# A Fourier transform feeding an MLP on one core: three folds and eight first-stage copies of batch 0 move to VectorE

## The chip, the core and the metric

The kernel runs on one core of a Trainium2 chip. The metric is the device time of one execution in microseconds; lower is better. The engines are TensorE (PE in the rows, with its weight loads as PEld), VectorE (DVE), ScalarE (ACT), GpSimd (POOL) and SyncE (SP), which here issues most DMAs. A trailing q (SPq, ACTq) is an engine's queue of DMA issues.

## The reference

Eight batches of 3008 x 256 go through a two-dimensional Fourier transform, of which the real part is kept, and then through a two-layer MLP with a piecewise activation:

```python
X = np.fft.fft(x, axis=1); X = np.fft.fft(X, axis=2)
x = X.real.reshape(8 * 3008, 256)
h = x @ w_in                                   # 256 x 2048
g = np.where(h >= 1, h, np.where(h <= -1, 0.0, (h + 1) ** 2 / 4))
out = g @ w_out                                # 2048 x 256
```

The weights come as 64-bit floats.

## The kernel before

The transform along the sequence is split into 47 x 64. Per batch there are eight inputs `x` of 96 x 2 x 512. **Stage one** (`stage1`, L258) multiplies each by a constant matrix on TensorE (L270) and writes the sums `s` into one PSUM bank per piece; four copies (L280) take each bank apart into the tile `z`, two for each half h of the partitions and each part m. `nyquist` (L285) computes `ny` from one column of `z`, copies it (`nyt`, L290) and sends it through DRAM (`nyr`, `nyb`). **Stage two** (`stage2`, L299) multiplies slices of the complete `z` (L309, PSUM tiles also named `s`) and splits each result into a high part `pqh` (ScalarE) and a low part `pql` (VectorE), both in `split` (L168). The transform along the columns is folded into `w_in`.

An input has two planes that are added. `fold_x` (L126) does the adding on GpSimd (L131, tile `y`) for all inputs of later batches and for the odd ones of batch 0; for the even ones of batch 0 TensorE gets both planes and accumulates twice as many matmuls. One float32 matmul leaves two records in the trace.

**Weights.** The 64-bit weights arrive as 16 blocks `raw`; `convert_w` (L192) makes float32 of a block by bit operations, mostly on VectorE (L210 to L225), with a conversion (L208) and, for some, a Relu (L215) on ScalarE. `fold_w_in` (L240) multiplies a pair of blocks by the column transform (`wps`, L246) and splits it into `wh` and `wl`; `fold_delta` (L249) makes `delta` from `dps` (L255); `split_w_out` makes `woh` and `wol`. Blocks 0 and 1 are converted first, then 4, 5, 2 and 3, and the others one by one between the units of the MLP.

**MLP.** A unit is one batch, one third of its columns and 128 of the 2048 features. `gemm1` (L350) makes `uv` on TensorE (L359), then `us` and two halves of `h` on VectorE (L362, L364, L365), `a` on ScalarE (L372, L373), `h` again on VectorE (L374), `gh` on ScalarE (L375) and `gl` on GpSimd (L378). `gemm2` (L382), four units later, adds to `acc` (L402). Batch 0 goes through the features in two visits, so that it can start before all weights are there.

**What sets the order.** `LOADS`, `START` and `NEXT` write out the beginning by hand (x an input's load, p a piece of the transform, c a conversion, f and d the folds of w_in and delta). A scheduler then places each engine's instructions by their dependencies and its own estimates, and puts in the waits; TensorE's order is kept as written within `START`. Each engine works strictly in its order, so an instruction that waits holds up what stands behind it. Tiles with one tag share a number of buffers, and a new tile waits until an old one is read.

Of the kernel before, what the change touches and what calls it, by code (L numbers as in the profile page):

```python
# [12 lines left out]
AF = mybir.ActivationFunctionType  # L13
ALU = mybir.AluOpType
# [84 lines left out]
CV = {0: ("gh", 4), 1: ("gh", 4), 4: ("gh", 4), 5: ("gh", 4), 2: ("a", 3), 3: ("h", 3)}  # L99


VECTOR_RELUS = (0, 1, 4, 5)

EARLY_BANKS = 24
# [5 lines left out]
def fft_ffn_kernel(ctx: ExitStack, tc: tile.TileContext, x, cst, w_in, w_out, out):  # L110
    nc = tc.nc
# [14 lines left out]
    def fold_x(b, q):  # L126

        t = xt.pop((b, q))
        if b or q % 2:
            y = sb.tile([96, CH], F32, tag="y", name=f"y_{b}_{q}", bufs=3)  # L130
            nc.gpsimd.tensor_tensor(y, t[:, 0], t[:, 1], op=ALU.add)  # L131
            yt[b, q] = [y]
        else:
            yt[b, q] = [t[:, 0], t[:, 1]]
        if q == 0:
            y = sb.tile([96, NA], F32, tag="yd", name=f"yd_{b}", bufs=1)
            nc.gpsimd.tensor_tensor(y, t[:, 0, :NA], t[:, 1, :NA], op=ALU.subtract)
            yt[b, "d"] = y
# [22 lines left out]
    def fft_bank(b, name):  # L161

        if b == 0 and early[0] < EARLY_BANKS:
            early[0] += 1
            return ps.tile([P, CH], F32, tag=f"acc{early[0] % 4}", name=name, bufs=1)
        return ps.tile([P, CH], F32, tag="fft", name=name, bufs=1)
# [25 lines left out]
    def convert_w(n):  # L192
# [15 lines left out]
        nc.scalar.activation(lowf, low, AF.Copy, scale=2.0**-52)  # L208
        if n in VECTOR_RELUS:
            nc.vector.tensor_scalar(exp, high, 20, 0x7FF, op0=ALU.logical_shift_right, op1=ALU.bitwise_and)  # L210
# [47 lines left out]
    def stage1(b, q):  # L258
        for p in range(q, min(q + 2, XC)):
            if (b, p) in xt and (b, p) not in yt:  # L260
                fold_x(b, p)
        if q == 0:
            zt[b] = sb.tile([P, NC, P + 1], F32, tag="z", name=f"z_{b}", bufs=1)
        z, y = zt[b], yt[b, q]
        bank = fft_bank(b, f"s1_{b}_{q}")
        pt = bank[:, : GPC * 96].rearrange("p (i n) -> p i n", i=GPC)
        for i in range(GPC):
            for j, part in enumerate(y):
                lhs = part[:, i * P : (i + 1) * P]
                mm = nc.tensor.matmul(pt[:, i], lhs, bm[:96, :], start=(j == 0), stop=(j == len(y) - 1))  # L270
                if i == 0:
                    pinned(b, mm)
        if q == 0:
            pd = bank[:NA, GPC * 96 : GPC * 96 + 2 * NC]
            nc.tensor.matmul(pd, yt[b, "d"], bm[:96, : 2 * NC], start=True, stop=True)  # L275
        for h in range(2):
            for m in range(2):
                src = pt[h * NA : (h + 1) * NA].rearrange("p i (t m c) -> p m c (i t)", t=2, m=2)[:, m]
                dst = z[m * NA : (m + 1) * NA, :, (2 * q + h) * 8 : (2 * q + h + 1) * 8]
                nc.scalar.activation(dst, src, AF.Copy)  # L280
        if q == 0:
            for m in range(2):
                nc.scalar.activation(z[m * NA : (m + 1) * NA, :, P], pd[:, m * NC : (m + 1) * NC], AF.Copy)
# [32 lines left out]
    def pinned(b, matmul):  # L316

        if b:
            tc.keep_in_program_order(matmul)

    def fft_pieces(b):
        pieces = []
        for q in range(XC):
            pieces.append((4, lambda q=q: stage1(b, q)))
        pieces.append((2, lambda: nyquist(b)))
        for h in range(NC // 4):
            pieces.append((4, lambda h=h: stage2(b, h)))
        return pieces
# [6 lines left out]
    for b in range(NB):  # L335
        visits = 1 if b else 2
        m = NFT // visits
# [86 lines left out]
    for _ in range(7):  # L424
# [4 lines left out]
    steps = {  # L429
        "x": lambda n: load_x(0, n),  # L430
        "y": lambda n: fold_x(0, n),
        "p": lambda n: first[n][1](),
        "l": load_w,
# [18 lines left out]
    for i in range(n_units + LAG):  # L452
        run_steps(STEPS.get(i, ""))
        if i < n_units:
            b, r = divmod(i, per)
# [75 lines left out]
```

## Time and profile before

| what | value |
|---|---|
| time, median of three runs | 1764.74 us (1764.58 to 1770.89) |
| the profiled execution, its time | 1765.38 us |
| its span in the trace | 1763.6 us |
| TensorE busy | 1735.8 us (98%) |
| VectorE busy | 1440.0 us (82%) |
| ScalarE busy | 1346.3 us (76%) |
| GpSimd busy | 1202.1 us (68%) |

Busy matmul time is modelled, so a full TensorE is not one at its peak. The start, up to about 200 us, in which weights are converted beside the MLP, looks different from the rest; the shares are averages over both.

### The profile page before, as it was taken

What the parts mean: (1) busy time and instruction counts of PE and PEld (TensorE: products, weight loads), DVE (VectorE), ACT (ScalarE), POOL (GpSimd) and SP (SyncE); (2) the same over time, 40 slices, a digit from 0 to 9 for tenths busy, and PEclk for the clock granted to TensorE, in tenths of its full rate; (3) what the DMA queues carried; (4) which work ended last, traced back from release to release, by engine and by line L of the source; (5) the groups of instructions that cost most, each with busy time, mean ns of one, the idle gap of its engine ahead of it and who ended that gap; (6) DMA issues with size and microseconds to landing.
All of it is one profiled execution on the core that took longest, in us unless ns stands there. A gap on an engine that the chain in (4) does not pass through costs nothing.

```text
span 1763.6 us, 21942 instructions
## 1 busy us (share of the span) xinstructions
PE 1735.8 (98%) x7982; PEld 1420.5 (81%) x7982; DVE 1440.0 (82%) x1766; ACT 1346.3 (76%) x1580; POOL 1202.1 (68%) x838
## 2 busy tenths in 40 slices
PE   9988999999999999999999999999999999999998
PEld 6766888888888788888888888888888888888877
DVE  6999788888887888878888788878888788888887
ACT  5777877777777877777778877788778787777776
POOL 1545966776768766787667876677676766667775
PEclk9999999999999999999999999999999999999999
DMA  7013321010010100110001100011000000000000
GB/s 230 12 66 101 101 104 60 28 50 30 13 51 28 53 30 1 51 48 33 30 10 51 50 28 24 22 39 50 28 24 34 1 23 32 11 25 5 19 25 24
DMA packets 29963, 72.51 MB, mean 41 GB/s; under 512 B 2976, under 2 KB 8224, under 8 KB 29856
## 3 DMA queue, kind: packets, MB, share of 16 engines
q1 hardware_dynamic: 29568, 70.08, 12.1%
q8 instruction: 62, 1.02, 0.2%
q10 hardware_dynamic: 288, 1.05, 0.2%
q14 instruction: 45, 0.37, 0.1%
HBM read 43.31 MB, written 27.81 MB: 40 GB/s over the span
## 4 chain that ended last, share of the span: by engine, by line
PE 61%; ACT 10%; POOL 9%; issue 6%; DVE 5%; ACTq 0%; POOLq 0%; DVEq 0%
PE acc L402 38%; PE uv L359 19%; POOL gl L378 9%; DVE h L374 4%; ACT a L373 4%; ACT gh L375 3%; ACT a L372 3%; PE s L270 2%; PE s L309 2%; ACT z L280 1%; DVE o L414 0%; DVE h L365 0%; DVE h L364 0%; POOL y L131 0%; ACT o L412 0%
## 5 line engine op out<-in xcount | busy, mean ns | idle before, releaser
L378 POOL TENSOR_TENSOR gl<-h,gh 128x512 fp32r<-128x512 f32 (+1 forms) x765 | 1095.1, 1454 | 513.3 <-ACT gh L375 491.7
L374 DVE SCALAR_TENSOR_TENSOR h<-a,h 128x1024 f32<-128x1024 f32 (+1 forms) x385 | 578.0, 1502 | 219.7 <-ACT a L373 218.1
L375 ACT ACTIVATE gh<-h 128x1024 fp32r<-128x1024 f32 (+1 forms) x385 | 400.6, 1041 | 356.9 <-DVE h L374 344.2
L402 PE MATMUL acc<-gh,woh 128*128 128x512 f32 (+1 forms) x1536 | 608.3, 396 | 6.7 <-ACT gh L375 3.3
L402 PE MATMUL acc<-gl,woh 128*128 128x512 f32 (+1 forms) x1536 | 604.6, 394 | 9.1 <-POOL gl L378 9.1
L402 PE MATMUL acc<-gh,wol 128*128 128x512 f32 (+1 forms) x1536 | 596.2, 388 | 0.0
L372 ACT ACTIVATE a<-h,biases 128x1024 f32<-128x1024 f32 (+1 forms) x385 | 431.7, 1122 | 10.0 <-DVE h L365 7.7
L373 ACT ACTIVATE a<-a 128x1024 f32<-128x1024 f32 (+1 forms) x385 | 398.8, 1036 | 7.1
L402 PEld LDWEIGHTS acc<-gl,woh 128*128 128x128 f32 x1536 | 288.8, 188 | 76.4 <-POOL gl L378 16.8
L402 PEld LDWEIGHTS acc<-gh,woh 128*128 128x128 f32 x1536 | 289.3, 188 | 68.9 <-DVE o L414 5.5
L402 PEld LDWEIGHTS acc<-gh,wol 128*128 128x128 f32 x1536 | 289.5, 188 | 59.2
L364 DVE TENSOR_TENSOR h<-us,uv 128x512 f32<-128x512 f32 (+1 forms) x384 | 259.3, 675 | 67.2 <-POOL gl L378 27.3
L359 PE MATMUL uv<-pqh,wh 128*128 128x512 f32 (+1 forms) x768 | 303.7, 395 | 3.0 <-DVE us L362 2.9
L359 PE MATMUL uv<-pql,wh 128*128 128x512 f32 (+1 forms) x768 | 301.4, 392 | 0.0
L359 PE MATMUL uv<-pqh,wl 128*128 128x512 f32 (+1 forms) x768 | 299.5, 390 | 0.0
L362 DVE SCALAR_TENSOR_TENSOR us<-nyb,delta,uv 128x512 f32<-128x512 f32 (+1 forms) x384 | 278.5, 726 | 14.6 <-PE uv L359 13.8
L365 DVE TENSOR_TENSOR h<-us,uv 128x512 f32<-128x512 f32 (+1 forms) x384 | 256.0, 667 | 0.0
L359 PEld LDWEIGHTS uv<-pqh,wh 128*128 128x128 f32 x768 | 144.4, 188 | 40.9 <-DVE us L362 6.8
L359 PEld LDWEIGHTS uv<-pql,wh 128*128 128x128 f32 x768 | 144.6, 188 | 32.1
L359 PEld LDWEIGHTS uv<-pqh,wl 128*128 128x128 f32 x768 | 144.4, 188 | 30.5 <-issue 0.2
L131 POOL TENSOR_TENSOR y<-x 96x512 f32<-96x512 f32 x60 | 106.4, 1774 | 20.0 <-DMA x<-in_x_dram 8.2
L280 ACT ACTIVATE z<-s 64x192 f32<-64x192 f32 x256 | 86.6, 338 | 6.5 <-PE s L275 1.7
(54 smaller groups left out, 548.0 us busy)
## 6 DMA issues: line engine op xcount, KB each, us to landing
x<-in_x_dram SPq DMA_DIRECT2D x64, 384.0 KB, 3.3
out_dram<-o SPq DMA_DIRECT2D x30, 512.0 KB, 2.8
out_dram<-o SPq DMA_DIRECT2D x16, 482.0 KB, 3.0
nyb<-nyr SPq DMA_DIRECT2D x24, 256.0 KB, 3.4
raw<-in_moe_w_out_dram SPq DMA_DIRECT2D x8, 512.0 KB, 10.9
raw<-in_moe_w_in_dram SPq DMA_DIRECT2D x6, 512.0 KB, 4.5
part<-o SPq DMA_DIRECT2D x4, 512.0 KB, 3.2
o<-part SPq DMA_DIRECT2D x4, 512.0 KB
```

The costliest lines, as they stand in the source:

```text
L131: nc.gpsimd.tensor_tensor(y, t[:, 0], t[:, 1], op=ALU.add)
L280: nc.scalar.activation(dst, src, AF.Copy)
L359: nc.tensor.matmul(t[:, :n], w[m][:, cols], r[:, m, :n], start=(j == 0), stop=(j == 2))
L362: nc.vector.scalar_tensor_tensor(us, nyb[b, k][:, :n], delta[:, f : f + 1], uv[0], op0=ALU.mult, op1=ALU.add)
L364: nc.vector.tensor_tensor(h[:, 0], us, uv[1], op=ALU.subtract)
L365: nc.vector.tensor_tensor(h[:, 1], us, uv[1], op=ALU.add)
L372: nc.scalar.activation(a[:, sl], h[:, sl], AF.Relu, bias=half, scale=0.5)
L373: nc.scalar.activation(a[:, sl], a[:, sl], AF.Square)
L374: nc.vector.scalar_tensor_tensor(h[:, sl], a[:, sl], 1.0, h[:, sl], op0=ALU.min, op1=ALU.max)
L375: nc.scalar.activation(gh[:, sl], h[:, sl], AF.Copy)
L378: eng.tensor_tensor(gl[:, sg], h[:, sg], gh[:, sg].bitcast(F32), op=ALU.subtract)
L402: nc.tensor.matmul(acc[:, :n], w[:, f, wc], g[:, sg], start=(first and j == 0), stop=(last and j == 2))
```

## The change

Inputs 4, 6 and 7 of batch 0 are folded on VectorE. Inputs 4 and 6 were not folded before (TensorE accumulated both planes), and input 7 was folded on GpSimd. Of the four copies of a first-stage bank in batch 0's pieces 4 to 7, the two with m = 1 go to VectorE; the two with m = 0 stay on ScalarE.

```diff
+VECTOR_FOLDS = (4, 6, 7)
+VECTOR_COPIES = 4
...
     def fold_x(b, q):
 
         t = xt.pop((b, q))
-        if b or q % 2:
+        if b or q % 2 or q in VECTOR_FOLDS:
+            engine = nc.vector if b == 0 and q in VECTOR_FOLDS else nc.gpsimd
             y = sb.tile([96, CH], F32, tag="y", name=f"y_{b}_{q}", bufs=3)
-            nc.gpsimd.tensor_tensor(y, t[:, 0], t[:, 1], op=ALU.add)
+            engine.tensor_tensor(y, t[:, 0], t[:, 1], op=ALU.add)
...
-                nc.scalar.activation(dst, src, AF.Copy)
+                if m and b == 0 and q >= VECTOR_COPIES:
+                    nc.vector.tensor_copy(dst, src)
+                else:
+                    nc.scalar.activation(dst, src, AF.Copy)
```

The scheduler moves other instructions along with these. In the rows below line numbers after the change are 4 higher up to the folds and 7 higher behind the copies (L285 is the new copy on VectorE, L287 ScalarE's). `s_0_6` and `s_0_7` with z are stage one's pieces 6 and 7, `s_0_0` to `s_0_2` with pqh or pql are stage two's; `raw_119`, `raw_121` and `raw_123` are blocks 4, 5 and 2; the trailing figures number tiles. What stands in brackets is the engine, or the DMA ring, for which an instruction waits.

VectorE, from the middle of block 5's conversion to the first two pql, before:

```order
L217 TENSOR_SCALAR cv_310<-raw_121 128x512
L223 TENSOR_SCALAR cv_310<-cv_310 128x512 [waits DVE_49]
L218 SCALAR_TENSOR_TENSOR cv_310<-cv_310,raw_121 128x512 [waits DVE_49,Activation_49]
L224 SCALAR_TENSOR_TENSOR cv_310<-raw_121,cv_310 128x512 [waits DVE_49]
L214 TENSOR_SCALAR cv_320<-raw_123 128x512 [waits DMAHW6_49]
L225 SCALAR_TENSOR_TENSOR cv_310<-cv_310 128x512 [waits DVE_49]
L170 TENSOR_TENSOR pql_0_286<-s_0_0_287,pqh_0_285 128x4x2x64 [waits Activation_49]
L217 TENSOR_SCALAR cv_320<-raw_123 128x512
L170 TENSOR_TENSOR pql_0_286<-s_0_1_294,pqh_0_285 128x4x2x64 [waits Activation_49]
```

And after, from the first copy of piece 7 on:

```order
L285 COPY z_137<-s_0_7_250 64x24x8 [waits Activation_49]
L285 COPY z_137<-s_0_6_241 64x24x8 [waits Activation_49]
L221 TENSOR_SCALAR cv_297<-raw_119 128x512
L227 TENSOR_SCALAR cv_297<-cv_297 128x512 [waits DVE_49]
L285 COPY z_137<-s_0_7_250 64x24x8 [waits Activation_49]
L222 SCALAR_TENSOR_TENSOR cv_297<-cv_297,raw_119 128x512 [waits DVE_49]
L228 SCALAR_TENSOR_TENSOR cv_297<-raw_119,cv_297 128x512 [waits DVE_49]
L214 TENSOR_SCALAR cv_306<-raw_121 128x512 [waits DMAHW5_49]
L229 SCALAR_TENSOR_TENSOR cv_297<-cv_297 128x512 [waits DVE_49]
L174 TENSOR_TENSOR pql_0_282<-s_0_0_283,pqh_0_281 128x4x2x64 [waits Activation_49]
L174 TENSOR_TENSOR pql_0_282<-s_0_1_290,pqh_0_281 128x4x2x64 [waits Activation_49]
L215 TENSOR_SCALAR cv_306<-cv_306 128x512 [waits DVE_49]
```

Before, blocks 4 and 5 were converted ahead of the first pql; now the last z copy stands in the middle of block 4, and block 5 (`cv_306`) comes behind both pql.

ScalarE, from the copies of piece 6 to the Relu of block 2 (L215), before:

```order
L280 ACTIVATE z_137<-s_0_6_241 64x24x8 [waits PE_49]
L280 ACTIVATE z_137<-s_0_6_241 64x24x8 x3
L280 ACTIVATE z_137<-s_0_7_254 64x24x8 [waits PE_49]
L280 ACTIVATE z_137<-s_0_7_254 64x24x8 x3
L256 ACTIVATE delta<-dps_263 128x4 [waits PE_49]
L290 ACTIVATE nyt_275<-ny_273 24x64 [waits PE_49]
L208 ACTIVATE raw_123<-raw_123 128x512 [waits DMAHW6_49]
L208 ACTIVATE raw_125<-raw_125 128x512 [waits DMAHW7_49]
L169 ACTIVATE pqh_0_285<-s_0_0_287 128x4x2x64 [waits DVE_49,PE_49]
L215 ACTIVATE cv_320<-cv_320,biases 128x512 [waits DVE_49]
```

And after:

```order
L287 ACTIVATE z_137<-s_0_6_241 64x24x8 [waits PE_49]
L287 ACTIVATE z_137<-s_0_7_250 64x24x8 [waits PE_49]
L287 ACTIVATE z_137<-s_0_6_241 64x24x8 [waits DVE_49]
L260 ACTIVATE delta<-dps_259 128x4 [waits PE_49]
L297 ACTIVATE nyt_271<-ny_269 24x64 [waits PE_49]
L212 ACTIVATE raw_123<-raw_123 128x512 [waits DMAHW6_49]
L287 ACTIVATE z_137<-s_0_7_250 64x24x8 [waits DVE_49]
L212 ACTIVATE raw_125<-raw_125 128x512 [waits DMAHW7_49]
L173 ACTIVATE pqh_0_281<-s_0_0_283 128x4x2x64 [waits PE_49,Activation_49]
L173 ACTIVATE pqh_0_281<-s_0_1_290 128x4x2x64 [waits PE_49]
L173 ACTIVATE pqh_1_380<-s_0_2_382 128x4x2x64 [waits DVE_49,PE_49,Activation_49]
L219 ACTIVATE cv_316<-cv_316,biases 128x512 [waits DVE_49]
```

ScalarE's last z copy went behind delta, nyt and a conversion, and the Relu went behind two further pqh. On TensorE half of the third stage-two piece (`s_0_2`) stands ahead of the first wps now, and its other half behind both wps of block 4 and the first unit's uv. SyncE's order is the same, GpSimd's lacks one fold, and behind the first unit's h all engines' orders are as before.

## Rows read from the trace of the kernel before

**Rows 1.** Busy time by stretch: from:to, length, PE, PEld, DVE, ACT, POOL, granted clock, DMA.

```profile
40.00:60.00 20.00, 16.85 (x86) 13.70 (x85) 19.16 (x30) 15.09 (x19) 8.62 (x6) 1.00 0.01 2
...
80.00:100.00 20.00, 17.01 (x67) 12.02 (x66) 19.04 (x28) 14.25 (x17) 11.29 (x8) 1.00 0.24 76
...
200.00:220.00 20.00, 18.86 (x93) 15.80 (x92) 15.51 (x19) 17.15 (x25) 19.07 (x14) 1.00 0.21 60
```

**Rows 2.** VectorE in order of time: start, length, operation, idle before and its releaser.

```profile
18.48 0.69 DVE L170 TENSOR_TENSOR wl<-wps,wh 128x512 fp32r<-128x512 f32 x1 [3.05 <-ACT wh L169]
...
20.80 0.42 DVE L210 TENSOR_SCALAR cv<-raw 128x512 uint32<-128x512 uint32 x1
...
25.89 0.68 DVE L224 SCALAR_TENSOR_TENSOR cv<-raw,cv 128x512 uint32<-128x512 uint32 x1
26.50 0.42 DVE L214 TENSOR_SCALAR cv<-raw 128x512 uint32<-128x512 uint32 x1
26.83 0.68 DVE L225 SCALAR_TENSOR_TENSOR cv<-cv 128x512 f32<-128x512 f32 x1
30.44 0.69 DVE L170 TENSOR_TENSOR pql<-s,pqh 128x512 fp32r<-128x512 f32 x1 [2.93 <-ACT pqh L169]
...
32.14 0.69 DVE L170 TENSOR_TENSOR pql<-s,pqh 128x512 fp32r<-128x512 f32 x1 [0.68 <-ACT pqh L169]
...
38.93 0.65 DVE L364 TENSOR_TENSOR h<-us,uv 128x482 f32<-128x482 f32 x1
39.50 0.65 DVE L365 TENSOR_TENSOR h<-us,uv 128x482 f32<-128x482 f32 x1
```

**Rows 3.** TensorE in order of time, same columns; xN counts records.

```profile
19.37 1.92 PE L270 MATMUL s<-cs,x 96*128 96x96 f32 x16
...
24.70 2.39 PE L255 MATMUL dps<-cs,cv 128*128 128x1 f32 x16
...
27.69 3.78 PE L309 MATMUL s<-cs,z 128*128 128x128 f32 x16 [0.26 <-ACT z L280]
31.27 2.59 PE L246 MATMUL wps<-cv,cm 128*128 128x512 f32 x4
...
33.92 0.38 PE L359 MATMUL uv<-pqh,wl 128*128 128x482 f32 x1
...
35.03 1.88 PE L246 MATMUL wps<-cv,cm 128*128 128x512 f32 x4
```

**Rows 4.** ScalarE in order of time, same columns.

```profile
24.86 2.78 ACT L280 ACTIVATE z<-s 64x192 f32<-64x192 f32 x8
...
27.84 1.20 ACT L208 ACTIVATE raw<-raw 128x512 f32<-128x512 uint32 x2
29.81 0.60 ACT L169 ACTIVATE pqh<-s 128x512 fp32r<-128x512 f32 x1 [0.77 <-PE s L309]
...
40.18 0.62 ACT L169 ACTIVATE woh<-cv 128x512 fp32r<-128x512 f32 x1
40.70 1.09 ACT L372 ACTIVATE a<-h,biases 128x964 f32<-128x964 f32 x1
```

**Rows 5.** GpSimd in order of time: the fold of input 5.

```profile
16.61 1.26 POOL L131 TENSOR_TENSOR y<-x 96x512 f32<-96x512 f32 x1 [1.73 <-DMA x<-in_x_dram]
```

**Rows 6.** VectorE's copy out of PSUM in time, and its smallest write (group: busy, mean ns).

```profile
83.92 0.66 DVE L414 COPY o<-acc 128x482 f32<-128x482 f32 x1 [0.35 <-PE acc L402]
...
L153 DVE MEMSET biases<- 128x1 f32 x2 | 0.1, 59 | 0.8 <-PEq L512 0.8
```

**Rows 7.** Single microseconds, columns as in rows 1: the granted clock stands third from the end.

```profile
25.00:26.00 1.00, 1.00 (x11) 1.00 (x10) 1.00 (x4) 0.96 (x4) 0.00 (x0) 0.93 1.05 389
...
32.00:33.00 1.00, 1.00 (x3) 0.50 (x2) 0.86 (x2) 0.11 (x1) 0.00 (x0) 0.66 0.92 293
...
129.00:130.00 1.00, 0.00 (x0) 0.00 (x0) 1.00 (x3) 0.83 (x1) 0.00 (x0) 1.00 0.99 406
...
132.00:133.00 1.00, 1.00 (x3) 0.80 (x3) 1.00 (x3) 0.25 (x1) 0.82 (x1) 0.50 1.04 336
```

## The prediction

> **What bounds the kernel now.** The shares of the whole span come first: TensorE is busy for almost all of it, and that says little about this change, since the build moves instructions only in the first 45 us. So I cut the span into stretches. Between 40 and 100 us VectorE is the full engine: it idles 0.84 of 20 us and 0.96 of 20 us, while TensorE idles about 3 us in each; from 200 us on TensorE is nearly full [rows 1]. Until then VectorE converts the weights beside its share of the MLP, and TensorE waits for what comes out. The end of the kernel is therefore the moment at which VectorE has worked off its early list, plus a length that the change doesn't touch.
>
> Next, VectorE's own order of time [rows 2]. It has three holes: 3.05 us before 18.48 (waiting for ScalarE's copy of the folded weights), 2.93 us before 30.44 and 0.68 us before 32.14 (both waiting for ScalarE's copy of a stage-two result). After 32.14 it runs through to the first h of the MLP at 38.93. The chain to the second hole is: TensorE's first stage of the pieces 4 to 7 from 19.37, dps from 24.70, stage two from 27.69, where it had waited for the last z copy [rows 3]; ScalarE's eight z copies of pieces 6 and 7 fill 24.86 to 27.64 [rows 4].
>
> **The change, part by part.** Times below are in the profiled execution (1765.38 us).
>
> *Fold of input 4.* Input 5 lands at 16.61 [rows 5] and the loads run in order, so input 4 is there before. The fold has two SBUF inputs of 512 elements; such an operation takes VectorE 0.61 us, from 25.89 to 26.50 [rows 2]. It falls into the hole before 18.48: cost 0. Without that hole it would cost its 0.61.
>
> *Folds of inputs 6 and 7.* In the built order they stand behind the copies wl, so behind 20.80: 2 x 0.61 = 1.2 us of new VectorE work.
>
> *Eight z copies.* The trace has no copy of 64x192 on VectorE. Above lies its copy of 128x482 out of PSUM, 0.66 us, of which 0.08 overlaps the next instruction, as between 25.89 + 0.68 and 26.50: 0.58. Below lies a one-element write of 0.06 [rows 2, 6]. By elements, 0.06 + 0.52 x 191/481 = 0.27; I take 0.28, so 8 x 0.28 = 2.2 us, with ends of 0.5 and 4.6. Added work on VectorE after 20.80: 3.4 us.
>
> *What TensorE saves.* Pieces 4 and 6 need 8 records instead of 16, at 0.11 each ((1.92 - 0.27)/15 [rows 3]): 16 x 0.11 = 1.8 us. ScalarE saves eight copies of 0.35, 2.8 us, and GpSimd one fold in a time when nothing else needs it. These gains count only if z is complete earlier. The built order decides that, and it says no. The copies of a piece alternate: each VectorE copy waits for the ScalarE copy ahead of it, and ScalarE's second waits for VectorE's first. In piece 7 ScalarE's second copy now stands behind delta, nyt and a conversion, so behind TensorE's dps and ny.
>
> The trace agrees with that alternation as far as it goes: the two readers of a stage-two bank, pqh on ScalarE from 29.81 for 0.60 and pql on VectorE from 30.44, follow each other [rows 2, 4]. [...]
>
> *When z is complete.* VectorE reaches its last copy at 20.80 + 7 x 0.28 + 2 x 0.61 + 4 conversions x 0.33 (26.50 to 26.83) + some 0.5 for the hand-overs (an estimate) = 25.8. Input 7 is folded at about 23.2 (three copies, two folds, part of the hand-overs); its matmuls end at 24.1; dps and ny took 24.70 to 27.43, 2.7 us [rows 3], so they end at 26.8. nyt thus ends near 27.0 instead of 27.9, and SyncE's nyr and nyb with it, for which nothing waited. ScalarE needs 0.20 for delta and nyt (27.64 to 27.84), 0.60 for the conversion and 0.35 for the copy [rows 4]: 28.0. VectorE's copy ends at 28.25, stage two starts at 28.3 instead of 27.69: **0.6 us later**, not earlier. VectorE has stood still from 25.8 to 28.0, 2.2 us, and queued behind its waiting copy are four conversions that the hole before 30.44 doesn't hide any longer as a whole.
>
> *From there to the MLP.* Those four take 3 x 0.61 + 0.33 = 2.2: 30.4. pql of the first half is due at 30.44 + 0.6, so 0.6 of idling; the second at 32.14 + 0.6 = 32.75, so 1.1 (before: 0.68). VectorE is free at 33.35 and has ten conversions ahead that stood before these waits until now: 6 x 0.33 + 4 x 0.61 = 4.4, to 37.8. The next one needs a Relu of ScalarE, which is now queued behind pqh of the third stage-two piece, and TensorE finishes that piece only behind wps, the first uv and a second wps. TensorE: 28.3 + 20 records x 0.21 (3.58 from 27.69 to 31.27, by 16, a little less) = 32.4; two wps records at the half clock, 0.86 each, twice the 0.43 of 35.03 (1.88 for four); six uv at 0.22 (33.92 to 35.03 for five); two wps at 0.43; dps and the rest of the piece 0.7: 37.0 [rows 3]. ScalarE's pqh and Relu add 0.7 and 0.65: 38.4. VectorE idles 0.6. That term hangs on the clock; between none and 2 us is possible.
>
> *Sum.* From 20.80 to the first h at 38.93 VectorE idled 2.93 + 0.68 = 3.6; now 0.5 + 2.2 + 0.6 + 1.1 + 0.6 = 5.0. Added work 3.4, added idling 1.4: the first h comes 4.8 later. About 0.5 is given back at once: before, ScalarE took h up at 40.70, 0.55 after its end at 40.15, because it was with woh (40.18 for 0.62) [rows 2, 4]; now both woh stand ahead of the end of h. That leaves **+4.3 us**. Behind it VectorE is full to 100 us, so nothing wins it back, and all later waits shift with it. TensorE's 1.8 us lie in a time in which it will wait anyway. 1765.38 + 4.3 = 1769.7; the profiled execution is 0.6 above the median of the runs, so against the median: **1769.0 us**, 0.24% more.
>
> The measurement can tell about 0.5% from no change, 8.8 us. The forecast is inside that.
>
> **Bounds.** Copies at 0.06 or 0.58 move the sum by -1.7 and +2.4, the Relu wait by -0.6 and +1.4: +2 to +8, 1767 to 1773. I stay at 4.3 because the copy is nearest in form to the PSUM copy of rows 6 and scales with its elements.
>
> **Rivals.**
> *The holes take it all.* Before, VectorE idled 3.6 us in this stretch, and the added work is 3.4. If the copies are short and TensorE catches up at the Relu, the list is done at its old time: 1764 to 1767. For it: the sum of the holes. Against it: the built order puts the new work ahead of the hole and conversions behind two waits, so that the hole appears again. 22%.
> *The start is shorter.* If TensorE and ScalarE, not VectorE, set the pace, their 1.8 us appear as gain: 1762.5 to 1763.5. Against it: VectorE's 0.84 us of idling in the 20 us that follow. 8%.
> *Slower by over 0.5%: the half clock comes a second time.* [...] Now TensorE will wait between 41 and 47 us for us, for h and for pql, with little to do between. If the clock falls there, 6.7 us at half cost 3.4 us of matmuls, in a stretch where the work behind is dense: 1772.4; with the first low stretch lengthened too, 1776. It decides over the 0.5% line once 4.5 us are lost beside the forecast's 4.3. Against it: before, TensorE waited there as well and the clock stayed up. 15%, 9% of it over the line.
> That the change doesn't do what it says is ruled out by the built order: the three folds and eight copies are on VectorE.
>
> **How the numbers follow.** Forecast 55%, the other three 22, 8 and 15. The likeliest gives 1769.0. Low end 1763.5 leaves out part of the second rival (6%), high end 1773.5 most of the third (10%). Faster by over 0.5%: 2%, since no term is as large; slower by over 0.5%: the 9% plus a little for the upper bounds, 10%; within: 88%.
>
> **What the profile after would show.** Fold of input 4 between 15.4 and 18.5, with no later wl: first step right. VectorE idling some 2 us ahead of its last z copy, with ScalarE as releaser, and stage two starting at 28 or later: right; at 26 or before: the third case. The first h at 43 to 44 and VectorE as full as before up to 100: the sum is right. The first h near 39: the holes took it. Granted clock at half between 41 and 50: the slow case. Copies far from 0.28 each, or a critical stretch that no longer runs through VectorE's early list, would make the forecast wrong.

## The result, and the profile after

| what | before, beside it | after |
|---|---|---|
| median | 1765.51 us | 1773.62 us (7 runs, 1770.60 to 1776.36) |
| ratio, with its 95% interval | | 1.0042 [1.0028, 1.0056] |
| the same kernel in a second comparison (e5 below) | 1764.47 us | 1772.65 us, ratio 1.0051 [1.0038, 1.0063] |
| profiled execution, its span | 1765.38, 1763.6 us | 1770.60, 1768.8 us |

The change makes the kernel 7.4 us slower by the ratio, where +4.3 was forecast. The profiled execution is the quickest of the seven, 3.0 us under their median; what it shows of the loss is therefore a lower end. Of all runs below, one of e11 (3691.31 us) counts as slow and is not in its ratio.

The windows of after, columns as in [rows 1] (from:to, length, busy time of PE, PEld, DVE, ACT, POOL, granted clock, DMA share, GB/s):

```profile
40.00:60.00 20.00, 15.99 (x69) 12.55 (x69) 17.58 (x28) 11.54 (x15) 4.22 (x4) 0.74 0.01 1
80.00:100.00 20.00, 17.28 (x73) 13.40 (x73) 19.49 (x28) 15.25 (x18) 10.74 (x9) 1.00 0.25 76
42.00:43.00 1.00, 0.94 (x3) 0.54 (x3) 1.00 (x3) 0.00 (x0) 0.00 (x0) 0.74 0.00 0
46.00:47.00 1.00, 0.57 (x2) 0.00 (x0) 1.00 (x3) 0.97 (x2) 0.00 (x0) 0.50 0.00 0
52.00:53.00 1.00, 1.00 (x7) 0.97 (x7) 0.59 (x1) 0.06 (x1) 1.00 (x2) 0.64 0.00 0
```

Two things have changed. From 40 to 60 us the mean granted clock is 0.74 where [rows 1] had 1.00: TensorE falls to half the clock (0.50 in the microsecond from 46) at about 42.5 and comes back at about 52.7 (between 1.00 and 0.50, a microsecond at a mean of 0.74 has 0.48 us at full speed, one at 0.64 has 0.28). And VectorE, full there before (19.16 of 20), now idles 2.4 us. From 80 on VectorE is full again and the clock is up.

VectorE of after in order of time (start, length, operation, idle before and its releaser):

```profile
15.48 0.68 DVE L135 TENSOR_TENSOR y<-x 96x512 f32<-96x512 f32 x1
18.61 0.69 DVE L174 TENSOR_TENSOR wl<-wps,wh 128x512 fp32r<-128x512 f32 x1 [2.45 <-ACT wh L173]
...
21.05 0.35 DVE L285 COPY z<-s 64x192 f32<-64x192 f32 x1
...
22.15 0.74 DVE L285 COPY z<-s 64x192 f32<-64x192 f32 x2
...
28.93 0.36 DVE L285 COPY z<-s 64x192 f32<-64x192 f32 x1 [2.19 <-ACT z L287]
...
32.21 0.69 DVE L174 TENSOR_TENSOR pql<-s,pqh 128x512 fp32r<-128x512 f32 x1 [0.66 <-ACT pqh L173]
33.46 0.69 DVE L174 TENSOR_TENSOR pql<-s,pqh 128x512 fp32r<-128x512 f32 x1 [0.55 <-ACT pqh L173]
...
43.74 0.64 DVE L371 TENSOR_TENSOR h<-us,uv 128x482 f32<-128x482 f32 x1
...
50.14 0.69 DVE L174 TENSOR_TENSOR pql<-s,pqh 128x512 fp32r<-128x512 f32 x1 [1.10 <-ACT pqh L173]
...
53.57 0.69 DVE L174 TENSOR_TENSOR pql<-s,pqh 128x512 fp32r<-128x512 f32 x1 [0.98 <-ACT pqh L173]
...
90.28 0.66 DVE L421 COPY o<-acc 128x482 f32<-128x482 f32 x1 [0.37 <-PE acc L409]
```

Read against [rows 2]: the fold of input 4 lies in the hole ahead of wl and costs nothing. The hole of 2.93 us has moved: 2.19 of it now stand ahead of the last z copy, in the middle of block 4. The first h comes at 43.74 instead of 38.93, **4.81 later**. The first copy of a result comes at 90.28 instead of 83.92 [rows 6], **6.36 later**. So 1.55 us were lost between them, where the forecast expected 0.5 to be given back. Of VectorE's 2.4 us of idling between 40 and 60, 2.1 are the two waits at 50.14 and 53.57, for pqh of stage-two pieces that TensorE makes at the low clock.

ScalarE of after shows what the last z copy waited for, and when a follows h:

```profile
27.43 0.17 ACT L260 ACTIVATE delta<-dps 128x4 f32<-128x4 f32 x1 [1.89 <-PE dps L259]
...
27.89 0.64 ACT L212 ACTIVATE raw<-raw 128x512 f32<-128x512 uint32 x1
28.55 0.34 ACT L287 ACTIVATE z<-s 64x192 f32<-64x192 f32 x1
...
44.98 1.10 ACT L379 ACTIVATE a<-h,biases 128x964 f32<-128x964 f32 x1 [0.51 <-DVE h L372]
```

VectorE's copy starts at 28.93, 0.04 after ScalarE's ends at 28.89. ScalarE had stood idle for 1.89 us ahead of delta, which waited for TensorE's dps and stands ahead of that copy. The a of the first unit is 4.28 late (44.98 against 40.70 [rows 4]).

TensorE of after:

```profile
24.64 2.76 PE L259 MATMUL dps<-cs,cv 128*128 128x1 f32 x16
...
29.43 3.80 PE L316 MATMUL s<-cs,z 128*128 128x128 f32 x20 [1.70 <-DVE z L285]
...
42.06 0.49 PE L366 MATMUL uv<-pqh,wh 128*128 128x482 f32 x1 [1.27 <-DVE us L369]
...
45.00 0.77 PE L366 MATMUL uv<-pqh,wh 128*128 128x482 f32 x1 [1.70 <-DVE h L372]
...
47.40 2.07 PE L316 MATMUL s<-cs,z 128*128 128x128 f32 x8 [0.83 <-DVE pql L174]
```

Stage two starts at 29.43, 1.74 later than in [rows 3]. The last three rows are the new thing: between 40.8 and 45.0 TensorE does three matmuls. Behind the first pause of 1.27 the clock falls (0.74 in the microsecond from 42), so that it is at half already in the second, of 1.70; the uv at 45.00 takes 0.77 instead of 0.49, the half piece at 47.40 2.07, where the same eight records took 1.16 before. In the kernel before, TensorE's two longest pauses between 40 and 46 us were shorter, and the clock stayed up:

```profile
42.60 1.16 PE L309 MATMUL s<-cs,z 128*128 128x128 f32 x8 [1.04 <-DVE pql L170]
44.70 0.49 PE L359 MATMUL uv<-pqh,wh 128*128 128x482 f32 x1 [0.94 <-DVE us L362]
```

### The profile page after: what moved, and what is told of

Read it like the earlier page. It is cut to its first block, busy times and chain, and to the rows that moved or that the text cites. A ratio compares the mean times of both kernels' runs of the same rounds, so it can differ in the third digit from the quotient of the medians.

```text
span 1768.8 us, 21906 instructions
## 1 busy us (share of the span) xinstructions
PE 1736.4 (98%) x7966; PEld 1420.7 (80%) x7966; DVE 1442.9 (82%) x1777; ACT 1344.2 (76%) x1572; POOL 1203.1 (68%) x837
## 4 chain that ended last, share of the span: by engine, by line
PE 82%; ACT 4%; DVE 2%; issue 2%; POOL 1%; ACTq 0%; POOLq 0%; DVEq 0%
PE acc L409 51%; PE uv L366 26%; PE s L274 2%; PE s L316 2%; DVE h L381 1%; ACT a L380 1%; ACT gh L382 1%; POOL gl L385 1%; ACT a L379 1%; ACT z L287 0%; DVE o L421 0%; DVE o L417 0%; DVE h L371 0%; ACT o L419 0%; PE ny L294 0%
## 5 line engine op out<-in xcount | busy, mean ns | idle before, releaser
L287 ACT ACTIVATE z<-s 64x192 f32<-64x192 f32 x248 | 84.1, 339 | 7.6 <-PE s L274 2.3
```

## The experiments

Theory: the loss is made on VectorE's early list, by the added work and above all by the waits that the new order puts into it, and is made larger by TensorE's second fall to half the clock. Rivals: the loss is the amount of VectorE work alone; it lies in the steady part; the clock makes all of it. Ratios are against the kernel before, run beside each. "First h" and "first o" are the starts of those VectorE rows in the profiled execution, of which there is one per kernel.

| kernel | first h | first o | clock 40 to 60 | ratio |
|---|---|---|---|---|
| before | 38.93 | 83.92 | 1.00 | |
| after | 43.74 | 90.28 | 0.74 | 1.0042 [1.0028, 1.0056] |
| e1 folds alone | 42.09 | 88.92 | 0.74 | 1.0032 [1.0021, 1.0043] |
| e2 copies alone | 42.47 | 89.27 | 0.74 | 1.0038 [1.0026, 1.0050] |
| e3 without piece 7's copies | 43.07 | 89.41 | 0.83 | 1.0046 [1.0034, 1.0058] |
| e4 after, TensorE kept busy | 43.37 | 88.93 | 1.00 | 1.0056 [1.0043, 1.0070] |
| e5 after again | 45.86 | 92.39 | 0.74 | 1.0051 [1.0038, 1.0063] |
| e6 as e4, fewer added | 45.26 | 90.02 | 1.00 | 1.0050 [1.0038, 1.0063] |
| e7 folds on GpSimd | 42.69 | 89.53 | 0.74 | 1.0034 [1.0022, 1.0046] |
| e8 before with added work | 40.99 | 87.15 | 0.91 | one run, 1767.85 us |
| e9 as e1, blocks 4 and 5 earlier | 41.63 | 87.58 | 0.83 | 1.0038 [1.0025, 1.0052] |
| e10 after, blocks 4 and 5 earlier | 47.84 | 94.72 | 0.83 | 1.0068 [1.0055, 1.0081] |
| e11 one fold on GpSimd, blocks earlier | 39.13 | 85.35 | 1.00 | 1.0018 [1.0009, 1.0028] |
| e12 as e9, w_out's split later | 39.92 | 86.76 | 0.91 | 1.0011 [1.0002, 1.0020] |

Not every difference in the first h is the edit's. The starts differ from execution to execution: VectorE's second wl, ahead of all moved work but the fold of input 4, starts at 20.20 in before and between 19.64 (e2) and 20.84 (e5) in the others, apart from e8 (24.20, by its edit) and e10 (22.55). And TensorE's first low stretch of the clock, around dps, lasts 6.8 us in before, after, e1, e4, e7, e9 and e11, but 10.2 in e3, e5, e6 and e12.

**e1, the folds alone.**

```diff
-VECTOR_COPIES = 4
+VECTOR_COPIES = 8
```

> Inputs 4, 6 and 7 are folded on VectorE; all first-stage copies stay on ScalarE. The work theory (each microsecond put on VectorE behind wl is paid, and order and waits on top): two folds, 1.2 us, less what the hole before the first pql still takes: the first h at 39.5 to 40.5 instead of 38.93, time 0.5 to 2 us above the kernel before, no second low stretch of the clock. The alternation theory (only the last z copy, which the copies' alternation puts behind delta and nyt, costs): first h at 38.9, time as before or 0.5 us less. If the folds are what costs, 4 us or more.

VectorE of e1:

```profile
24.23 0.69 DVE L222 SCALAR_TENSOR_TENSOR cv<-cv,raw 128x512 f32<-128x512 uint32 x1 [0.86 <-ACT raw L212]
...
29.80 0.69 DVE L174 TENSOR_TENSOR pql<-s,pqh 128x512 fp32r<-128x512 f32 x1 [2.33 <-ACT pqh L173]
...
31.51 0.69 DVE L174 TENSOR_TENSOR pql<-s,pqh 128x512 fp32r<-128x512 f32 x1 [0.42 <-ACT pqh L173]
...
39.65 0.69 DVE L174 TENSOR_TENSOR wol<-cv,woh 128x512 fp32r<-128x512 f32 x1 [1.37 <-ACT woh L173]
```

Only 1.2 us of work (two folds) come behind 20.8, and stage two is earlier by 0.6 (pql at 29.80, 30.44 in [rows 2]). Yet the first h is 3.16 later: the waits add up to 0.86 + 2.33 + 0.42 + 1.37 = 5.0 instead of 3.6. The new one, 1.37, is that of wol. It stood ahead of h before as well, at 36.50, and didn't wait there; what has moved is ScalarE's woh, which now stands behind a pqh, both wh and delta. Before, then e1:

```profile
35.68 0.63 ACT L169 ACTIVATE woh<-cv 128x512 fp32r<-128x512 f32 x1 [0.57 <-DVE cv L225]
```

```profile
39.00 0.62 ACT L173 ACTIVATE woh<-cv 128x512 fp32r<-128x512 f32 x1
```

So the loss isn't the amount of work alone.

**e2, the copies alone.**

```diff
-VECTOR_FOLDS = (4, 6, 7)
+VECTOR_FOLDS = ()
```

> Eight first-stage copies on VectorE, no fold of the inputs 4 and 6 there and input 7's on GpSimd. The work theory: 8 x 0.36 = 2.9 us of new work plus the hand-overs of the alternation: first h at 42 to 43.5, 3 to 4.5 us later, and if TensorE then starves between 41 and 47, a second low stretch with another 2 us: time +3 to +6.5 us. The alternation theory says nearly the same as the full change, first h at 43.7 and +5 us, with an idle of VectorE of about 2 us ahead of the last z copy. If the folds cost and the copies don't: +1 us or less.

The first h is 3.54 later, by eight copies (2.8) and longer waits. VectorE of e2 shows the same stall as after, in two parts:

```profile
27.17 0.36 DVE L285 COPY z<-s 64x192 f32<-64x192 f32 x1 [1.38 <-ACT z L287]
27.77 0.36 DVE L285 COPY z<-s 64x192 f32<-64x192 f32 x1 [0.24 <-ACT z L287]
```

And wol waits for woh here too, 0.86. Folds alone 3.16 and copies alone 3.54 make 6.7, both together 4.81: the parts share waits and don't add up. By the medians, too, either alone costs most of the loss.

**e3, piece 7's copies back on ScalarE.**

```diff
-                if m and b == 0 and q >= VECTOR_COPIES:
+                if m and b == 0 and VECTOR_COPIES <= q < XC - 1:
```

> The change, but the four copies of piece 7 all on ScalarE, so that no VectorE copy stands behind delta and nyt: VectorE's work falls by 2 x 0.36 = 0.7 us and the idle of 2.19 us ahead of the last z copy goes. The alternation theory: most of the loss goes with that stall, first h at 40.8 to 41.5 and the time 1 to 2.5 us above the kernel before. The work theory: VectorE runs ahead only to wait for pqh instead (the hole comes back at the first pql, whose bank needs all of z), so that only the 0.7 us of copies and what stage two gains come back: first h at 42 to 43, time 3 to 5 us above before. If a second low stretch of the clock remains between 41 and 52, 2 us of the loss remain with it.

The stall ahead of the last copy shrinks, and the next one grows. VectorE of e3:

```profile
26.18 0.36 DVE L285 COPY z<-s 64x192 f32<-64x192 f32 x1 [0.94 <-ACT z L287]
...
31.76 0.69 DVE L174 TENSOR_TENSOR pql<-s,pqh 128x512 fp32r<-128x512 f32 x1 [3.22 <-ACT pqh L173]
```

h is 0.67 earlier than in after, for two copies fewer (0.74). By that the wait of 2.19 isn't a cost of its own: VectorE waits for stage two in one place or in another. The ratio, no lower than that of after, agrees; the trace alone doesn't settle it, since the first low stretch was 3.4 us longer in this execution, and e5 below shows that such a start can cost some 2 us.

**e4, e6 and e5: the clock.** In e4 and e6 TensorE gets matmuls between 40 and 48 us whose results nobody reads (e4 has four more, on wl); e5 is after again, on the chip of e6.

```diff
+    def fill(count, lhs, rhs, bank="acc1"):
+        t = ps.tile([P, CH], F32, tag=bank, name="fill", bufs=1)
+        for _ in range(count):
+            nc.tensor.matmul(t[:, : rhs.shape[-1]], lhs, rhs, start=True, stop=True)
...
+        if f4 == 1:
+            fill(6, wh[1][:, CH : CH + P], wh[1][:, CH : 2 * CH], "acc0")
...
+        if i == 0:
+            fill(3, us[:, :P], us)
...
+        if i == 0:
+            fill(1, h[:, 0, :P], h[:, 0])
```

> The change with matmuls added whose results nobody reads: six on wh, three on us, one on h and four on wl, in the time between 40.8 and 48 us in which TensorE stands still for VectorE; the order of everything else is the changed kernel's. [...] The rival (VectorE alone sets the pace here, TensorE's clock is of no account): same time as the changed kernel, and the lateness at 60 us stays 6.3. If the added matmuls themselves hold up uv or s, 1 us slower.

> The changed kernel once more, as the measure for the runs beside it. Both theories: 7 us above the kernel before, 5 to 10; first h at 43.7 to 43.8, lateness 4.3 us there. If the second low stretch of the clock (42.7 to 52.6 in the first profile) came by chance of that execution alone, the profile now shows the clock up from 33 on and a lateness of 4.3 to 4.5 at 60 us; if it belongs to the waiting of TensorE, it is there again and the lateness at 60 is 6.3.

> The change with matmuls added between 40.8 and 47 us whose results nobody reads, as before but without the four on wl, which in the last run held back the second half of stage two's third piece from 47.0 to 47.96. The clock theory: no low stretch between 40 and 60, lateness 4.1 to 4.5 us at 60 instead of 6.3, and the time 1.5 to 2.5 us under the changed kernel's of the same comparison. The rival (the clock is of no account for the time): lateness 6 at 60 all the same, or the time equal to the changed kernel's within 1 us.

One microsecond of e5, then of e6, columns as in the windows above:

```profile
46.00:47.00 1.00, 0.00 (x0) 0.00 (x0) 1.00 (x3) 0.61 (x1) 0.00 (x0) 0.50 0.00 0
```

```profile
46.00:47.00 1.00, 1.00 (x4) 0.39 (x3) 1.00 (x3) 0.50 (x1) 0.00 (x0) 1.00 0.00 0
```

With TensorE busy the clock is 1.00 there and, by the table, in the whole stretch; in e5 it is 0.50. From the first h to the first o takes 44.76 us in e6 and 46.53 in e5: the low stretch costs **1.8 us** by then. The other kernels with VectorE's old order behind h agree in the main: 44.99 in before and 45.56 in e4 at a mean clock of 1.00; 46.16 in e8 at 0.91; 45.95 in e9 at 0.83; 46.54 to 46.84 in after, e1, e2 and e7 at 0.74. (In e3 and e10 one more operation stands behind the first h, in e11 and e12 the order is another.)

But the medians of e4 and e6 aren't lower than those of after. In their profiled executions TensorE fell to half the clock again later (at 97.9 in e4; at 99.2 and 170.9 in e6), and in e4 the steady part lost more (below). The fall in e4 takes back what the fill had won: the lateness of VectorE's h against before goes from 5.0 us at 98 to 6.8 at 109 (times of before). It doesn't need the fill: e3 (at 98.3), e9 (97.1) and e12 (99.1) have such a fall too, and after, e1, e2, e5 and e7, whose stretch between 40 and 60 is the longest, don't. What decides between them stays open. The clock's cost by 90 us is shown; that it is still there at the end isn't.

e5 shows a second thing. Its first low stretch lasts to 34.4 (32.2 in after, both from the granted clock of single microseconds), stage two is later, and h comes at 45.86: two executions of one kernel differ by 2.1 us in the start.

**e7, the same folds on GpSimd.** Inputs 4 and 6 are folded as in after, but by GpSimd, and input 7 as before; VectorE gets no added work at all.

```diff
-VECTOR_FOLDS = (4, 6, 7)
-VECTOR_COPIES = 4
+VECTOR_FOLDS = ()
+VECTOR_COPIES = 8
...
-        if b or q % 2 or q in VECTOR_FOLDS:
+        if b or q % 2 or q in (4, 6) or q in VECTOR_FOLDS:
```

> The kernel before, but inputs 4 and 6 folded on GpSimd as the odd ones are, so that TensorE has half the records there and VectorE nothing new; copies all on ScalarE. If VectorE's added work is what costs: stage two starts 1.2 to 1.8 us earlier, VectorE's waits for pqh shrink, first h at 37.5 to 38.9, time 0 to 1.5 us under the kernel before. If the order costs (the scheduler now expects the first pql early and puts conversions of blocks 4 and 5 behind it): first h at 39.5 to 41, time 1 to 4 us above before, although no work was added to VectorE.

VectorE of e7, then GpSimd:

```profile
21.42 1.28 DVE L214 TENSOR_SCALAR cv<-raw 128x512 uint32<-128x512 uint32 x1
22.62 1.49 DVE L221 TENSOR_SCALAR cv<-raw 128x512 uint32<-128x512 uint32 x1
...
29.30 1.29 DVE L222 SCALAR_TENSOR_TENSOR cv<-cv,raw 128x512 f32<-128x512 uint32 x2 [2.12 <-ACT raw L212]
...
40.25 0.69 DVE L174 TENSOR_TENSOR wol<-cv,woh 128x512 fp32r<-128x512 f32 x1 [1.50 <-ACT woh L173]
```

```profile
21.15 2.67 POOL L135 TENSOR_TENSOR y<-x 96x512 f32<-96x512 f32 x2 [2.78 <-PE s L274]
```

h is 3.76 later without any added VectorE work. Two conversions that take 0.42 take 1.28 and 1.49 while GpSimd folds, 1.9 us in all, and 2.12 and 1.50 are waits for ScalarE. GpSimd's folds come only at 21.15, since y has three buffers and they wait 2.78 us for TensorE to have read one. Neither theory had h this late (41 at most).

**e8, added work in the kernel before.** Nine additions on VectorE, whose result nobody reads, in the first call of the w_in fold, ahead of wl.

```diff
+        if f4 == 0:
+            spare = sb.tile([P, CH], F32, tag="us", name="spare", bufs=2)
+            for _ in range(9):
+                nc.vector.tensor_tensor(spare, w[0], w[1], op=ALU.add)
```

> The kernel before with nine additions of 128x512 on VectorE whose result nobody reads, eight ahead of the first wl and one between the two, 9 x 0.61 = 5.5 us; all other instructions stand in the order of before. The hole of 3.05 us and the one ahead of the second wl take 4.2 of it, so that everything behind wl comes 1.3 us later. If added work is paid as such: first h at 40.2 and the time 1 to 1.5 us up. If work ahead of the first pql is hidden as long as the order stays: the idle of 2.93 us ahead of the first pql shrinks to 1.6, first h stays at 38.9 to 39.0, and the lateness at 60 us is 0.

VectorE of e8:

```profile
14.48 8.61 DVE L251 TENSOR_TENSOR spare<-cv,cv 128x512 f32<-128x512 f32 x8
...
24.81 0.42 DVE L210 TENSOR_SCALAR cv<-raw 128x512 uint32<-128x512 uint32 x1
...
32.80 0.69 DVE L170 TENSOR_TENSOR pql<-s,pqh 128x512 fp32r<-128x512 f32 x1 [1.28 <-ACT pqh L169]
```

The eight took 8.6 us beside GpSimd's folds, a mean of 1.08 each where the ninth took 0.68, so the list starts 4.0 late (24.81 against 20.80) and not the amount aimed at. h is 2.06 late. Half of a delay of 4.0 is taken up by the holes when nothing else is reordered; but pql is later as well (32.80), so the run doesn't separate the two, and I draw nothing firmer from it.

**e9, e10 and e11: blocks 4 and 5 converted earlier.** The order written out by hand is changed. e9 is the folds alone, e10 the whole change, with the first line below; e11 folds input 4 on VectorE, 6 and 7 on GpSimd, without copies, with the second.

```diff
-START = "p0 p1 c0 p2 p3 c1 f0 p4 p5 p6 p7 d0 p8 p9 p10 c4 c5"
+START = "p0 p1 c0 p2 p3 c1 f0 p4 p5 c4 p6 p7 d0 c5 p8 p9 p10"
```

```diff
-START = "p0 p1 c0 p2 p3 c1 f0 p4 p5 p6 p7 d0 p8 p9 p10 c4 c5"
+START = "p0 p1 c0 p2 p3 c1 f0 c4 c5 p4 p5 p6 p7 d0 p8 p9 p10"
```

> The three folds on VectorE and all copies on ScalarE, as in the run with the folds alone (5.7 us over the kernel before, first h at 42.09), but with the conversions of blocks 4 and 5 written into the hand-made start between the pieces 5 and 6 and behind d0, which brings them back ahead of the first pql and the first Relu ahead of the third pqh. The work on VectorE is the same. If the order made the loss: VectorE idles about 1.5 us instead of 5.0 between wl and the first h, first h at 38.3 to 39.5, no low clock between 40 and 53, time within 1.5 us of the kernel before. If the added work makes it: first h at 41 or later again and 4 to 6 us lost.

> The whole change with the same edit of the hand-made start. The work on VectorE is the changed kernel's, 4.2 us more than before behind wl; the last z copy of piece 7 still stands behind delta and nyt on ScalarE. If the order made the loss: the conversions fill the wait ahead of the last z copy, idle 1 to 2 us in all, first h at 40.5 to 41.5 instead of 43.74, and 2 to 4 us over the kernel before instead of 7 to 9. If added work is what is paid, first h at 43 or later and 6 us or more.

> The kernel before with input 4 folded on VectorE (in the hole ahead of the first wl) and input 6 on GpSimd, all copies on ScalarE, and the conversions of blocks 4 and 5 written ahead of piece 4 in the hand-made start. TensorE has 16 records less, VectorE nothing new behind wl. If the order is what counts: the first pql comes 0.5 to 1.2 us earlier, first h at 37.5 to 38.7, and the time is 0.5 to 1.5 us under the kernel before, which would make it the fastest. If GpSimd's folds hold up VectorE's conversions, as in the run with the folds on GpSimd, where two of them took 1.28 and 1.49 instead of 0.42: first h at 39 to 40.5, 0 to 3 us over.

VectorE of e9, and ScalarE of e9:

```profile
37.45 0.68 DVE L228 SCALAR_TENSOR_TENSOR cv<-raw,cv 128x512 uint32<-128x512 uint32 x1
40.42 0.69 DVE L174 TENSOR_TENSOR wol<-cv,woh 128x512 fp32r<-128x512 f32 x1 [2.29 <-ACT woh L173]
```

```profile
39.27 0.60 ACT L173 ACTIVATE pqh<-s 128x512 fp32r<-128x512 f32 x1 [0.89 <-PE s L316]
39.76 0.62 ACT L173 ACTIVATE woh<-cv 128x512 fp32r<-128x512 f32 x1
```

At 38.13 VectorE has everything done, us too, which e1 does only at 40.86; but it stands for 2.29 us in front of wol, and only wol and one conversion lie between it and h. ScalarE's woh is queued behind a pqh that waits for TensorE. The time that the new order wins goes into that wait: ahead of h the waits add up to 5.1, in e1 to 5.0.

VectorE of e10:

```profile
34.62 0.36 DVE L285 COPY z<-s 64x192 f32<-64x192 f32 x1 [1.94 <-ACT z L287]
...
40.12 0.69 DVE L174 TENSOR_TENSOR pql<-s,pqh 128x512 fp32r<-128x512 f32 x1 [2.81 <-ACT pqh L173]
```

What was meant to help makes it the slowest kernel: the conversions now stand between the copies and folds that TensorE needs, the last copy comes at 34.62 instead of 28.93, and pql 7.9 us later than in after. Not all of this is the order's doing: 2.2 of the 7.9 are there at wl already (22.55 against 20.33), and the clock was at half from 15.9 to 19.3 and from 26.1 to 39.8. The theory missed that the change could make it worse.

In e11 the first h is nearly where it was (39.13), but GpSimd's folds again hold up two conversions (1.23 and 1.49), and the median is above that of before.

**e12, w_out's split behind the first h.** e9, with one step of the hand-written order moved by a unit.

```diff
-    0: "o2",
-    1: "f1 d1 o3 p11",
+    0: "",
+    1: "o2 f1 d1 o3 p11",
```

> As the run with the three folds and early conversions (first h at 41.63, of which 2.29 are VectorE waiting at wol for ScalarE's woh), but with the split of the first two blocks of w_out written behind the first unit, so that wol stands behind both h. VectorE's work is the same, 1.2 us more than before behind wl. If a wait ahead of the first h is the price, not the work: VectorE comes to the first h at 38.0 to 38.8, before or with the kernel before (38.93), ScalarE takes h up at 40.4 to 41.1, TensorE idles under 1.3 us at a time between 40 and 46, its granted clock stays up there, and the time is within 2 us of the kernel before. If the work is paid: first h at 40 or later and 4 us or more over before. If what stands behind h in the new order (pql behind the second pass over h) costs instead: first h at 38 to 39, but 3 us or more lost by 60 us.

VectorE of e12, and TensorE:

```profile
31.85 0.69 DVE L174 TENSOR_TENSOR pql<-s,pqh 128x512 fp32r<-128x512 f32 x1 [2.52 <-ACT pqh L173]
...
39.92 0.65 DVE L371 TENSOR_TENSOR h<-us,uv 128x482 f32<-128x482 f32 x1
...
42.29 0.69 DVE L174 TENSOR_TENSOR wol<-cv,woh 128x512 fp32r<-128x512 f32 x1 [0.56 <-ACT woh L173]
```

```profile
46.65 1.16 PE L316 MATMUL s<-cs,z 128*128 128x128 f32 x8 [3.62 <-DVE pql L174]
```

The start of this execution is 1.8 us later than e9's (pql at 31.85 against 30.05), and still h is 1.7 earlier: the wait in front of h is gone. The same three folds on VectorE as in e1 and e9 now cost 1.0011 instead of 1.0032 and 1.0038, with intervals that don't meet: most of the folds' price went with one step of the order. Three reservations stand against more. The edit puts wol's own 0.6 us behind h, where the kernel before has it ahead, and that kernel was not run with the same edit. How the medians come to part by 4.8 us isn't seen in the traces: at the first o e12 is only 0.8 ahead of e9, and its profiled execution (1770.92) is the slowest of its eleven, above e9's (1769.84). And for the copies no run brings the old order back. The expectation held for the time (1.9 us by the ratio); but h came at 39.92, not at 38.0 to 38.8, TensorE's pause has moved behind the first unit (3.62), and the clock fell to half behind it, from 47.9 to 51.3. No version was faster than the kernel before.

**The steady part.** Nothing of the change lies there, yet lateness isn't constant. Some of VectorE's h behind the ScalarE step take 1.1 us longer while GpSimd's gl runs, in some executions and not in others. The kernel before, then after, at the same place of the program:

```profile
342.28 2.56 DVE L374 SCALAR_TENSOR_TENSOR h<-a,h 128x964 f32<-128x964 f32 x1 [0.89 <-ACT a L373]
```

```profile
348.62 1.45 DVE L381 SCALAR_TENSOR_TENSOR h<-a,h 128x964 f32<-128x964 f32 x1 [0.90 <-ACT a L380]
```

In after it is GpSimd that is held up at this place: one gl of these three takes 2.22 us, where the two in before take 1.22 each:

```profile
347.75 4.76 POOL L385 TENSOR_TENSOR gl<-h,gh 128x482 fp32r<-128x482 f32 x3
```

After wins 1.1 us here and once more some 14 us later; its lateness falls from 6.3 to 4.1 by 364 us and ends at 5.2. The odd one is the profile of before: of the fourteen, only e11 has a long h at the first place too (2.58) and only e10 at the second (2.55). In e4 it goes the other way: the lateness is 4.6 there and 9.3 at the end. So one profile differs from the median of its kernel by a few microseconds for a reason that has nothing to do with the change.

## Why the prediction was right and wrong

*What bounds the kernel: right.* The loss arises on VectorE's early list, and the windows from 80 us on are as before.

*The sum up to the first h: right, by parts that offset each other.* Forecast 4.8, measured 4.81; that it agrees so closely is luck. The copies were mis-sized: 0.35 to 0.37 each, so 8 x 0.37 = 3.0, not 2.2. That is inside the bounds of 0.06 and 0.58. The folds cost what was forecast (0 and 1.2). The waits came out smaller: 2.19, 0.66 and 0.55 make 3.4 (forecast 2.2, 0.6 and 1.1), and the Relu wait of 0.6 didn't appear: VectorE came there later, by what the copies had cost more. The list started 0.25 late (21.05 against 20.80), and 0.25 + 3.0 + 1.2 + (3.4 - 3.6) leaves 0.6 for the hand-overs, forecast at 0.5. So in after the waits ahead of h add up to no more than before; what the order does there is keep them from taking up the new work of 4.2 us, which is paid in full. Only where the folds stand alone (e1) do the waits themselves grow, to 5.0.

*When z is complete: right in kind, short by 1.1 us.* The last copy ended at 29.3 (forecast 28.25), stage two began at 29.43 (28.3). TensorE waited for VectorE's folds of inputs 6 and 7 first, so that dps began at 24.64 and not at 24.1, and dps took 2.76, not 2.39, with the clock at half from 25.4 on (25.9 in the kernel before).

*0.5 given back: right.* a is 4.28 late, forecast 4.3.

*"Nothing wins it back, and all later waits shift with it": this step failed.* The rest did not just shift. TensorE, short of work while VectorE was late, paused for 1.27 us, and its clock fell to half, for 10.2 us; and VectorE, which was to be as full as before up to 100, idles 2.4 of the 20 us from 40 on. This was the third rival, at 15%, and a fall between 41 and 51 came in every profile of the change and of its parts (after, e1, e2, e3, e5), and in e7, e8, e9, e10 and e12. Its argument against, "before, TensorE waited there as well and the clock stayed up", compared no lengths: the pauses before were 1.04 and 0.94. Its price was put too high (3.4) and came out as 1.8 at 90 us. The profiled execution is 6.36 late there, 2.1 more than the 4.28 at a; of that, e5 against e6 shows 1.8 to be the clock's. The rival's total, 1772.4, came nearer to the result than the forecast's 1769.0, but not by its own sum: 4.3 and 1.8 make 6.1 of the 7.4 us, and the rest is open. (Its 6.7 us at half are the length of the first low stretch in the kernel before, by [rows 7] from 25.86 to 32.68, so 6.8; the second in after lasted 10.2.)

*From 6.4 to the median.* Between the profiled execution, late by 5.2 at its end, and the median lie 3.0 us. e5 shows one source, a longer first low stretch, with h 2.1 later; the steps of 1.1 us in the steady part are another. How much of the 3.0 each makes wasn't measured. In the forecast this had no term, because the 0.6 between profile and median of the kernel before was carried over; against the seven runs beside the change that profile lies 0.1 under the median.

*The range.* It ended at 1773.5, the result is 1773.62, the repetition 1772.65. The range was set against 1764.74 for the kernel before, which ran at 1765.51 beside the change; 1764.74 x 1.0042 is 1772.2, inside. 0.42% and 0.51% slower lie on the two sides of the line of 0.5%, so the 88% on the inside was too sure of it: the bounds of the single terms left out both the clock's cost and the differences from one execution to the next.

*The other rivals.* The holes did not take the work, since the order puts the holes elsewhere. The shorter start did not come: stage two began later, as the alternation of the copies demands. The rows that were named for this alternation say nothing of it, since pql reads pqh and has to follow it in any case; after shows two copies one behind the other (28.89, 28.93), in an order that the scheduler's waits set.

## What to carry to other kernels

Price an instruction that goes to another engine by its own time and by the waits that come with it into a queue worked in order: list what stands behind each new wait, and what the instructions ahead of the one that matters now wait for (in e1 the wait for wol, whose woh the scheduler had moved back on ScalarE, was 1.37 us, more than two folds at 1.2). Here a delay on the engine that feeds TensorE became a longer pause on TensorE (1.27 and 1.70 us instead of 1.04 and 0.94), with 10.2 us at half the clock: compare the pauses' lengths with those before, and add a low stretch of the clock as a term where they grow. With one profile against a loss of some microseconds, look for steps elsewhere in the program that differ by execution before the difference is explained.

## What the runs showed of the hardware

- VectorE and GpSimd took longer beside each other. Conversions of 0.42 us took 1.23 to 1.49 beside GpSimd's folds (e7, e11), additions of 0.68 a mean of 1.08 (e8), an h of 1.45 took 2.56 (before, at 342 us). Which of the two is longer differs between executions of one order: h 2.56 and gl 1.22 in before, 1.45 and 2.22 in after. What decides it, no run shows.
- A copy of 64x192 out of PSUM took VectorE 0.35 to 0.37 us, ScalarE 0.34 to 0.35: moving it gains nothing in itself.
- TensorE's granted clock fell behind or within a pause of 1.27 us in after and of 1.97 to 2.94 in e1, e2, e3, e7 and e9, all between 39 and 45 us, and not behind 1.04 and 0.94 in the kernel before; where the pauses were filled (e4, e6), it stayed up. Elsewhere it was less regular: a pause of 1.35 us ahead of the same uv was followed by the half clock in e4 (pause to 96.41, clock 0.50 from 98), and not in after (pause to 97.76) or before (pause to 91.41). No length of a pause that brings the fall can be read from these runs.
